# Queries loaded with twelve rows of a head to a partition: a new token order in an attention and gated-MLP kernel

## The chip, the core and the metric

The kernel runs on one core of one Trainium2 chip. The core has engines that run side by side, each with its own queue of instructions in order: TensorE (PE, with weight loads shown as PEld) multiplies matrices into PSUM, VectorE (DVE), ScalarE (ACT) and GpSimd (POOL) work element by element, and SyncE (SP) issues DMAs. ACT and POOL issue some DMAs too. Sixteen DMA engines move the data between HBM and SBUF. The metric is the device time of one execution in microseconds (us).

## The reference

Inputs are float32. q is [8, 16, 384, 64] (batch, query heads, tokens, head width), k and v are [8, 4, 384, 64], so four query heads share a key head. What is computed, per batch:

```python
scores = scale * np.matmul(q, k.transpose(0, 1, 3, 2))     # k, v repeated for 4 query heads
attn = softmax(scores); attn_out = np.matmul(attn, v)
x = attn_out.transpose(0, 2, 1, 3).reshape(B, S, H * D)    # [8, 384, 1024]
h = np.maximum(x @ w_in, 0.0)                              # w_in 1024 x 1024
u, v = h[..., :512], h[..., 512:]
v_n = (v - mean(v)) / sqrt(var(v) + 1e-6)                  # over the last axis
v_s = einsum('ts,bsd->btd', w_spatial, v_n) + b_spatial[None, :, None]   # mixes tokens
out = (u * v_s) @ w_out                                    # [8, 384, 1024]
```

The softmax and the sum over keys do not depend on the order in which keys stand. The token order of the queries is carried through x, h and v_n to the rows of the output, and w_spatial and b_spatial are indexed by it.

## The kernel before

**Tokens.** 384 tokens are three tiles of 128. Every load puts tokens 3p, 3p+1 and 3p+2 of a head in partition p (`(p t) d`, `part`, line 106): one partition then reads 768 contiguous bytes per head. Token tile t holds the tokens 3p+t. The output rows (line 447), the bias and w_spatial (`load_spatial`, `cast_spatial`, lines 498 to 509) use the same order.

**Stages.** A batch is 36 units: six sets s (token tile qt = s // 2, head group j = s % 2), each with three key tiles, and in each unit two matmuls that share the array, one for either half of the head pair (`units`, line 242, matmul at 256). For each, ScalarE takes the exponential into aT (`exp`, line 266); `weigh` (line 270) multiplies by v, with a column of ones for the sums, and VectorE divides (lines 289, 291). x is transposed (`x_turn` on TensorE for the first batches, `x_send` by DMA from batch 2). `gated` (line 455) is a generator of the MLP's matmuls: `v_part` (pv, line 331), `u_part` (pu, 390), `s_part` (psp with wsT16, 409), `o_part` (po, 436, copy to osb, store at 450 or 452). `pour` (line 612) takes these as filling between the attention's units; the Python code thus writes the order of TensorE's queue out by hand. In the first 21 units (`ALONE`, line 631) one unit is emitted at a time, later three.

**The start.** k, q and v are loaded as float32 and cast to float16, then turned by TensorE transposes for batches 0 and 1 (`k_turn`, `q_turn`), by DMA transposes from batch 2 (`k_send`, `q_send`). Lines 124 to 129 issue the first loads: half of the first q tile on ACT's queue, the others on SP's. Lines 533 to 541 are what the engines do first, with groups of matmuls on an identity matrix (`idle`, line 525) between the transposes. Lines 543 to 569 give POOL's order of casts and DMA issues: w_in, the loads of batches 1 and 2, the bias, w_spatial, w_out. `at(n, ...)` hangs work on unit n; lines 570 to 588 hang the first transposes there.

**Queues.** SP issues in order: first loads, the transpose of w_spatial (line 512), then batch by batch the loads, the transposes of k, q and x, and the output stores. `osb` has three buffers, which hold one batch's three token tiles.

Of the kernel before, what the change touches and what calls it, by code (L numbers as in the profile page):

```python
# [9 lines left out]
FP32 = mybir.dt.float32  # L10
# [7 lines left out]
def kernel(  # L18
# [75 lines left out]


    stage = {}

    def stage_tile(n, b, j=None):
        heads = 2 * G if n == "q" else HKV
        t = ld.tile(  # L100
            [P, heads, NT * D], FP32, name=f"{n}32_{b}_{j}", tag=f"{n}32", bufs=4 if n == "q" else 2
        )
        stage[n, b, j] = t
        return t
# [7 lines left out]
    def load_v(b, eng=sp):  # L112
        part(v[b], stage_tile("v", b), 0, HKV, eng)

    def load_q(b, j, eng=sp):
        part(q[b, 8 * j : 8 * j + 8], stage_tile("q", b, j), 0, 2 * G, eng)

# [5 lines left out]
    )  # L123
    part(q[0, 0:8], q00, G, 2 * G, act)
    part(k[0], k0, 0, 2, sp)
    part(q[0, 0:8], q00, 0, G, sp)
    part(k[0], k0, 2, 4, sp)
    part(q[0, 8:16], q01, 0, 2 * G, sp)
    part(v[0], v0, 0, HKV, sp)

    w_in16 = cst.tile([P, NK, DFF], FP16, name="w_in16")
# [41 lines left out]
    def cast_q(b, j, eng, ts=None, hs=(0, 1)):  # L173
        if (b, j) not in q16s:
            q16s[b, j] = ld.tile([P, NT, G, 2, D], FP16, name=f"q16_{b}_{j}", tag="q16", bufs=4)
        t16 = q16s[b, j]
        src = stage["q", b, j].rearrange("p (h i) (t d) -> p h i t d", h=2, t=NT)
        for hh in hs:
            if ts is None:
                eng.tensor_copy(  # L180
                    t16[:, :, :, hh, :].rearrange("p t i d -> p i t d"), src[:, hh]
                )
            else:
                for t in ts:
                    eng.tensor_copy(t16[:, t, :, hh, :], src[:, hh, :, t])

# [55 lines left out]
    def units(u, count):  # L242
# [11 lines left out]
        for kt, hh, sc in sorted(scs, key=lambda x: x[:2]):  # L254
# [3 lines left out]
                kTs[b][rows, j, kt * P : (kt + 1) * P],  # L258
                qTs[b, j][rows, qt, :],
                start=True,  # L260
# [168 lines left out]
    def o_part(b, tt, half):  # L429
# [16 lines left out]
        cols = slice(half * 512, (half + 1) * 512)  # L446
        rows = out[b].rearrange("(p t) d -> p t d", t=NT)
        copy(act if half and (last or tt == 1) else dve, osb[:, cols], po, f"po_{b}_{tt}_{half}")
        if last:
            sp.dma_start(rows[:, tt, cols], osb[:, cols])  # L450
        elif half:
            sp.dma_start(rows[:, tt, :], osb)
        yield C512
# [66 lines left out]
    def at(n, f, *args):  # L520
        todo.setdefault(n, []).append((f, args))
# [47 lines left out]
    send_spatial()  # L569
    at(2, k_turn, 0, 1, dve)  # L570
    for n, b, j, t in (
        (2, 0, 1, 0),
# [10 lines left out]
    ):  # L583
        at(n, q_turn, b, j, t, dve)
    at(15, k_turn, 1, 0, dve)
    at(18, k_turn, 1, 1, dve)
# [127 lines left out]
```

## Time and profile before

| | us |
|---|---|
| median of three runs (244.82 to 245.74) | 244.94 |
| the profiled execution, its own time | 245.65 |
| its span in the trace | 243.5 |
| TensorE busy | 234.7 |
| ScalarE busy | 170.0 |
| VectorE busy | 142.6 |
| GpSimd busy | 99.3 |
| first scores (line 256) | 7.72 |
| last output store issued (line 450) | 240.24 |

The granted TensorE clock was 0.997 of full speed. The profile shows, for each group of instructions, the source line, the engine, out and in tiles, how often it ran, the mean time of one, and what the engine waited for before it. SPq is SP's queue of DMA issues; the time to landing of a DMA runs from its issue to the last byte's signal. q1 is the queue of DMAs that SP issues, q10 that of ACT, q0 that of POOL. A DMA share is the mean busy share of the 16 engines; it can go over 1 where packets of two queues overlap.

### The profile page before, as it was taken

Reading aid. Unit: us, or ns where it says so; the run is one execution under the profiler, and the core shown is the slowest. Engines: PE = TensorE matmul, PEld = TensorE weight load, DVE = VectorE, ACT = ScalarE, POOL = GpSimd, SP = SyncE. Lnnn points to the kernel's source line nnn. Section 1 sums busy time; section 2 is a strip of 40 time slices with the busy share of each in tenths; the row PEclk is TensorE's granted clock in tenths of the full one; section 3 lists DMA queues with packets and bytes.
Section 4 is the critical chain, followed back from the end, with each engine's and each line's share of the span. In section 5 each row is a group of like instructions: output and inputs, shape, how many; then the busy total and the mean of one; then the engine's idle time right before and its main releaser. Section 6 shows DMA issues by size and latency. Waiting matters only on the chain.

```text
span 243.5 us, 5905 instructions
## 1 busy us (share of the span) xinstructions
PE 234.7 (96%) x2334; PEld 126.3 (52%) x2334; DVE 142.6 (59%) x373; ACT 170.0 (70%) x348; POOL 99.3 (41%) x142
## 2 busy tenths in 40 slices
PE   7599999999999999999999999999999999999993
PEld 7355556645564545554555545645555545545541
DVE  1255866567545776367664766456754766467361
ACT  2599977977898868996888856977678866501211
POOL 1699872475042630349005830556003400360520
PEclk9999999999999999999999999999999999999998
DMA  7999999995399959996999399995932334240147
GB/s 218 241 270 285 301 323 204 154 319 195 63 145 264 276 168 215 239 250 223 203 239 265 109 187 247 321 187 113 227 88 43 106 112 132 43 172 3 61 192 265
DMA packets 70651, 46.68 MB, mean 192 GB/s; under 512 B 44912, under 2 KB 65456, under 8 KB 70624
## 3 DMA queue, kind: packets, MB, share of 16 engines
q1 hardware_dynamic: 66016, 37.27, 63.5%
q0 software_dynamic: 4080, 8.65, 14.7%
q8 instruction: 18, 0.29, 0.5%
q10 hardware_dynamic: 528, 0.39, 0.5%
q14 instruction: 9, 0.07, 0.1%
HBM read 25.95 MB, written 12.58 MB: 158 GB/s over the span
## 4 chain that ended last, share of the span: by engine, by line
PE 91%; DMA 3%; DVE 3%; SPq 1%; issue 0%; ACT 0%
PE pu L390 18%; PE po L436 17%; PE pv L331 17%; PE sc L256 15%; PE av L276 14%; PE psp L409 7%; DMA q<-in_q_dram 3%; PE xps L308 1%; PE qps L217 1%; DVE x L291 1%; SPq L107 1%; DVE qT L195 1%; DVE r L289 0%; DVE stats L357 0%; DVE vr L345 0%
## 5 line engine op out<-in xcount | busy, mean ns | idle before, releaser
L268 ACT ACTIVATE aT<-sc 128x512 f16<-128x512 f32 x288 | 148.0, 613 | 36.8 <-PE sc L256 36.2
L276 PEld LDWEIGHTS <-aT 128*128 128x128 f16 x1152 | 47.8, 97 | 17.3 <-issue 1.8
L375 POOL TENSOR_SCALAR vn<-vr,rstd,nmr 128x512 f16<-128x512 f32 x24 | 18.1, 767 | 85.6 <-DVE nmr L370 63.5
L276 PE MATMUL av<-v,aT 128*128 128x65 f16 x1152 | 51.6, 193 | 0.3 <-DVE x L291 0.2
L331 PE MATMUL pv<-w_in,xt 128*128 128x512 f16 x192 | 51.1, 379 | 0.0
L436 PE MATMUL po<-w_out,gT 128*128 128x512 f16 x192 | 50.7, 379 | 0.0
L390 PE MATMUL pu<-xt,w_in 128*128 128x384 f16 x256 | 49.9, 326 | 0.0
L256 PE MATMUL sc<-qT,kT 64*128 64x512 f16 x288 | 42.7, 380 | 0.8 <-DVE qT L195 0.7
L291 DVE TENSOR_TENSOR x<-av,r 128x256 f16<-128x256 f32 x96 | 40.7, 424 | 3.3
L422 POOL TENSOR_TENSOR gT<-vs,uT 128x384 f16<-128x384 f32 x31 | 28.2, 913 | 35.3 <-DVE vs L421 18.0
L289 DVE RECIPROCAL r<-av 128x4 f32<-128x4 f32 x96 | 17.2, 179 | 42.1 <-PE av L276 41.9
L195 DVE COPY osb<-po 128x512 f32<-128x512 f32 x38 | 25.9, 685 | 17.2 <-PE po L436 16.2
L390 PEld LDWEIGHTS <-w_in 128*128 128x128 f16 x256 | 22.1, 97 | 17.1 <-issue 5.5
L401 ACT ACTIVATE uT<-pu 128x384 f16<-128x384 f32 x32 | 15.8, 494 | 16.3 <-PE pu L390 16.2
L436 PEld LDWEIGHTS <-gT 128*128 128x128 f16 x192 | 17.1, 97 | 17.5 <-issue 3.0
L331 PEld LDWEIGHTS <-xt 128*128 128x128 f16 x192 | 16.0, 97 | 17.7 <-issue 5.3
L180 POOL CAST q<-q 128x768 f16<-128x768 f32 x28 | 22.4, 834 | 5.0 <-DMA q<-in_q_dram 4.2
L256 PEld LDWEIGHTS <-kT 64*128 64x128 f16 x288 | 10.8, 94 | 24.9 <-issue 13.5
L409 PE MATMUL psp<-wsT,vn 128*128 128x384 f16 x96 | 22.3, 327 | 0.0
L421 DVE TENSOR_TENSOR vs<-psp,bias_bc 128x384 f32<-128x384 f32 x32 | 17.6, 552 | 6.4 <-PE psp L409 6.3
L345 DVE TENSOR_SCALAR vr<-pv 128x512 f32<-128x512 f32 x24 | 16.4, 682 | 8.4 <-PE pv L331 8.4
L357 DVE BATCH_NORM_STATS2 stats<-vr 128x6 f32<-128x512 f32 x24 | 16.4, 685 | 0.1
(42 smaller groups left out, 100.4 us busy)
## 6 DMA issues: line engine op xcount, KB each, us to landing
out_dram<-osb SPq DMA_DIRECT2D x21, 512.0 KB, 2.7
q<-in_q_dram SPq DMA_DIRECT2D x11, 768.0 KB, 7.7
q<-in_q_dram POOLq DMA_DIRECT2D x4, 768.0 KB, 9.8
v_None<-in_v_dram SPq DMA_DIRECT2D x6, 384.0 KB, 4.5
w_in<-in_moe_w_in_dram POOLq DMA_DIRECT2D x4, 512.0 KB, 8.4
k_None<-in_k_dram SPq DMA_DIRECT2D x5, 384.0 KB, 4.0
out_dram<-osb SPq DMA_DIRECT2D x6, 256.0 KB, 2.4
w_out<-in_moe_w_out_dram POOLq DMA_DIRECT2D x2, 512.0 KB, 14.1
```

The costliest lines, as they stand in the source:

```text
L180: eng.tensor_copy(t16[:, :, :, hh, :].rearrange("p t i d -> p i t d"), src[:, hh])
L195: (act.copy if eng is act else dve.tensor_copy)(o, i)
L256: nc.tensor.matmul(sc, kTs[b][rows, j, kt * P : (kt + 1) * P], qTs[b, j][rows, qt, :], start=True, stop=True,)
L268: act.activation(a, sc, AF.Exp, scale=scale)
L276: nc.tensor.matmul(av[:, i * (D + 1) : (i + 1) * (D + 1)], aT[:, kt, hh, i * P : (i + 1) * P], v1[b % 2][:, 2 * j + hh, kt, 0 : D + 1], st ...
L291: dve.tensor_tensor(x16s[b][:, qt, c : c + 256].rearrange("p (i d) -> p i d", i=G), o[:, :, 0:D], r.to_broadcast([P, G, D]), ALU.mult,)
L331: nc.tensor.matmul(pv, xts[b][:, kt, st * P : (st + 1) * P], w_in16[:, kt, DH:DFF], start=(kt == 0), stop=(kt == NK - 1),)
L375: pool.tensor_scalar(vn, v_r.pop((b, st)), rstd[:, st : st + 1], nmr[:, st : st + 1], op0=ALU.mult, op1=ALU.add,)
L390: nc.tensor.matmul(pu[:, 0:S], w_in16[:, kt, m * P : (m + 1) * P], xts[b][:, kt, :], start=(kt == 0), stop=(kt == NK - 1),)
L409: nc.tensor.matmul(psp[:, 0:S], v_n[b, st][:, m * P : (m + 1) * P], wsT16[:, st, :], start=(st == 0), stop=(st == NT - 1),)
L422: (dve if b == B - 1 and m == NM - 1 else pool).tensor_tensor(gTs[b][:, m, :], vs, uTs[b][:, m, :], ALU.mult)
L436: nc.tensor.matmul(po, gTs[b][:, m, tt * P : (tt + 1) * P], w_out16[:, m, half * 512 : (half + 1) * 512], start=(m == 0), stop=(m == NM - 1),)
```

## The change

Queries get a new layout. Partition (i, c) now holds twelve rows of head i of a group of four: token 12c + 4t + r for t in 0..2 and r in 0..3, so that the whole group of four heads is 128 partitions of 3,072 contiguous bytes. Token tile t of the queries then holds tokens 12c + 4t + r with position (r, c). `part_q` loads any choice of half groups and token tiles: for the first batch, tile 0 of the first and second q tile is loaded ahead of v, and tiles 1 and 2 of both behind v. In the transposed q the columns of a tile stand as (r, i, c); the score matmul reads them in the order (i, r, c), in runs of 32. Keys and values keep their order. The output rows, the bias and w_spatial follow the new token order, so the output's DRAM side is walked as (r, c, d) and w_spatial's as (r, c, t, s).

The order at the start changes too. The group of 18 idle matmuls becomes 8; the cast of the second q tile on VectorE moves behind the second k transpose's copy, with 16 idle matmuls ahead of that q tile's transposes and 8 behind; on POOL the first half load of w_in's second column half and the cast of v are moved ahead of a q cast, and the second half load stands behind that cast.

```diff
     def stage_tile(n, b, j=None):
-        heads = 2 * G if n == "q" else HKV
+        shape = [P, 2, NT, G * D] if n == "q" else [P, HKV, NT * D]
...
+    def part_q(b, j, hs, ts, eng):
+        h0, h1, t0, t1 = hs[0], hs[-1] + 1, ts[0], ts[-1] + 1
+        eng.dma_start(
+            stage["q", b, j][:, h0:h1, t0:t1],
+            q[b, 8 * j + 4 * h0 : 8 * j + 4 * h1].rearrange(
+                "(h i) (c t r) d -> (i c) h t (r d)", i=G, t=NT, r=G
+            )[:, :, t0:t1],
+        )
+
     def load_q(b, j, eng=sp):
-        part(q[b, 8 * j : 8 * j + 8], stage_tile("q", b, j), 0, 2 * G, eng)
+        stage_tile("q", b, j)
+        part_q(b, j, (0, 1), (0, 1, 2), eng)
...
-    part(q[0, 0:8], q00, G, 2 * G, act)
+    part_q(0, 0, (1,), (0,), act)
     part(k[0], k0, 0, 2, sp)
-    part(q[0, 0:8], q00, 0, G, sp)
+    part_q(0, 0, (0,), (0,), sp)
     part(k[0], k0, 2, 4, sp)
-    part(q[0, 8:16], q01, 0, 2 * G, sp)
+    part_q(0, 1, (0, 1), (0,), sp)
     part(v[0], v0, 0, HKV, sp)
+    part_q(0, 0, (0, 1), (1, 2), sp)
+    part_q(0, 1, (0, 1), (1, 2), sp)
...
-        src = stage["q", b, j].rearrange("p (h i) (t d) -> p h i t d", h=2, t=NT)
+        src = stage["q", b, j].rearrange("p h t (r d) -> p h t r d", d=D)
...
-                qTs[b, j][rows, qt, :],
+                qTs[b, j][rows, qt].rearrange("p (r i c) -> p i r c", r=G, i=G),
...
-        rows = out[b].rearrange("(p t) d -> p t d", t=NT)
+        rows = out[b].rearrange("(c t r) d -> t r c d", t=NT, r=G)[tt]
...
-            sp.dma_start(rows[:, tt, cols], osb[:, cols])
+            sp.dma_start(rows[:, :, cols], osb[:, cols])
         elif half:
-            sp.dma_start(rows[:, tt, :], osb)
+            sp.dma_start(rows, osb)
...
-        eng.dma_start(ws32, moe_w_spatial.rearrange("(p t) s -> p t s", t=NT))
+        rows = moe_w_spatial.rearrange("(c t r) s -> r c t s", t=NT, r=G)
+        eng.dma_start(ws32, rows)
...
-            bias_bc.rearrange("a (t p) -> a t p", t=NT), b32.rearrange("a (p t) -> a t p", t=NT)
+            bias_bc.rearrange("a (t r c) -> a t r c", t=NT, r=G),
+            b32.rearrange("a (c t r) -> a t r c", t=NT, r=G),
...
-                ws16[:, :, tt, :], ws32[:, tt].rearrange("p (s t) -> p t s", t=NT)
+                ws16[:, :, tt].rearrange("p s (r c) -> p s r c", r=G),
+                ws32[:, tt].rearrange("p (c s r) -> p s r c", s=NT, r=G),
...
-    idle(18)
+    idle(8)
     q_turn(0, 0, 0, dve)
     idle(8)
 
-    cast_q(0, 1, dve, (0,))
+    load_w_in(1, 0, 4)
+    cast_v(0, pool)
     cast_q(0, 0, pool, (1,))
-    load_w_in(1, 0, 4)
     load_w_in(1, 4, 8)
-    cast_v(0, pool)
     cast_q(0, 1, pool, (1,))
...
     at(2, k_turn, 0, 1, dve)
+    at(2, cast_q, 0, 1, dve, (0,))
+    at(2, idle, 16)
...
+    at(2, idle, 8)
```

More of the change, by code (lines that the diff above doesn't have):

```diff
@@ L98, in stage_tile @@
     def stage_tile(n, b, j=None):
-        heads = 2 * G if n == "q" else HKV
+        shape = [P, 2, NT, G * D] if n == "q" else [P, HKV, NT * D]
         t = ld.tile(
-            [P, heads, NT * D], FP32, name=f"{n}32_{b}_{j}", tag=f"{n}32", bufs=4 if n == "q" else 2
+            shape, FP32, name=f"{n}32_{b}_{j}", tag=f"{n}32", bufs=4 if n == "q" else 2
         )
@@ L176, in cast_q @@
         t16 = q16s[b, j]
-        src = stage["q", b, j].rearrange("p (h i) (t d) -> p h i t d", h=2, t=NT)
+        src = stage["q", b, j].rearrange("p h t (r d) -> p h t r d", d=D)
         for hh in hs:
             if ts is None:
-                eng.tensor_copy(
-                    t16[:, :, :, hh, :].rearrange("p t i d -> p i t d"), src[:, hh]
-                )
+                eng.tensor_copy(t16[:, :, :, hh, :], src[:, hh])
             else:
                 for t in ts:
-                    eng.tensor_copy(t16[:, t, :, hh, :], src[:, hh, :, t])
+                    eng.tensor_copy(t16[:, t, :, hh, :], src[:, hh, t])
     def new_kT(b):
```

## The prediction

> **What bounds the kernel now.** I read the page's busy shares, the chain that ended last and the DMA parts first, then the timeline of the first 12 us, then the DMA queue's own timeline, and at last windows of one batch each.
>
> ```profile
> PE 234.7 (96%) x2334; PEld 126.3 (52%) x2334; DVE 142.6 (59%) x373; ACT 170.0 (70%) x348; POOL 99.3 (41%) x142
> ...
> PE 91%; DMA 3%; DVE 3%; SPq 1%; issue 0%; ACT 0%
> ...
> out_dram<-osb SPq DMA_DIRECT2D x21, 512.0 KB, 2.7
> q<-in_q_dram SPq DMA_DIRECT2D x11, 768.0 KB, 7.7
> ```
>
> TensorE is the bound: busy for 96% of the 243.5 us, and 91% of the chain. Only the start (the DMA share of the chain) and the last stores are not matmuls. The last lines are the loads and stores whose shape this change alters.
>
> The start, from the timeline (start, length, engine, line):
>
> ```profile
> 5.76 0.50 DVE L185 CAST q<-q 128x256 f16<-128x256 f32 x2 [1.58 <-DMA q<-in_q_dram]
> ...
> 7.72 0.82 PE L256 MATMUL sc<-qT,kT 64*128 64x512 f16 x6 [0.16 <-DVE qT L195]
> 8.13 3.04 ACT L268 ACTIVATE aT<-sc 128x512 f16<-128x512 f32 x6 [2.87 <-PE sc L256]
> ...
> 9.98 0.49 DVE L185 CAST q<-q 128x256 f16<-128x256 f32 x2 [2.41 <-DMA q<-in_q_dram]
> 10.39 0.35 DVE L195 COPY kT<-kps 128x384 f16<-128x384 f16 x1
> ...
> 11.87 7.11 ACT L268 ACTIVATE aT<-sc 128x512 f16<-128x512 f32 x14 [0.70 <-PE sc L256]
> ```
>
> Scores begin at 7.72, ScalarE at 8.13. From there to about 31 us ScalarE is nearly full (two exps of 0.51 us per unit), so the first exp sets this stage; its one real gap is 0.70 us, for the second q tile, whose load lands at 9.95.
>
> The end, from the DMA queue's timeline, and the queue's traffic in the window 229.5 to 232.6, which holds the first of these stores:
>
> ```profile
> 229.68 6.11 SPq L452 DMA_DIRECT2D out_dram<-osb  x3
> 236.06 4.51 SPq L450 DMA_DIRECT2D out_dram<-osb  x6
> ```
> ```profile
> q1 hardware_dynamic: 144, 0.52, 42.0%
> ```
>
> Nine stores go out in the last 11 us; the last is issued at 240.24 and lands at 242.3. In the window one store of 512 KB is 128 data packets of 4 KB: 0.42 x 16 engines x 3.1 us / 128 = 0.163 us for one packet on one engine, so 8 packets each, 1.3 us of its 2.6 us to landing. The other 1.3 us is fixed.
>
> One batch each, from the windows (time of each engine; the last two columns are DMA share and GB/s):
>
> ```profile
> 85.00:112.00 27.00, 27.00 (x276) 13.69 (x273) 16.80 (x45) 21.92 (x46) 9.45 (x14) 1.00 0.92 218
> 166.00:193.00 27.00, 27.00 (x273) 14.15 (x271) 16.34 (x43) 20.66 (x44) 8.04 (x11) 1.00 0.56 126
> ```
>
> A batch takes 27 us. Its DMA work fills 0.56 x 27 = 15 us of each DMA engine with stores and transposes alone, 25 us with the loads: hidden, but there is little room.
>
> **The change part by part.**
>
> *Head.* Ahead of the first q cast the old order moves 384 + 192 + 384 KB (landing at 5.74), the new one 128 + 192 + 128. Landings of the old loads follow each other at about 320 KB/us (384 KB from 4.55 to 5.74). The first q tile then lands near 4.2, bounded by a small load's own 2.9 us from issue. K's cast ends by 4.1, the two q casts (0.50) by 4.7. But eight idle matmuls at 0.118 us (18 took 2.13) run until 5.5 behind the k transposes, where 18 ran until 6.67. Four transposes (0.4 to 0.5), the copy (0.42): scores at about 6.5 instead of 7.72, so 1.2 us. The second q tile lands by 5.5. Its cast moves behind the k copy on VectorE, so the copy no longer waits 1.9 us in the queue; 16 idle matmuls (0.076 each when warm: 8 took 0.61) end about when that cast does. The gap of 0.70 shrinks to about 0.3. Head: 1.6 us gained; bounds 0 (DMA contention from w_in, issued two us sooner on POOL) and 2.3 (the whole gap goes too). SP issues two DMAs more, 0.5 us each, behind v: nobody waits for SP before 33 us. POOL's v cast now stands ahead of a q cast and the second w_in issue, which moves from 8.48 to about 10.4; at its old 7.5 us to landing it is there at 18, its first matmul comes at 20.64 less 1.6. The 14 idle matmuls more lie in waits. I take -1.6.
>
> *Casts and transposes* keep their counts and element numbers: nothing. Cover: POOL is 41% busy.
>
> *Scores* read q in runs of 32 columns (64 bytes). No matmul of before reads its moving operand in pieces. Bounds: nothing, or half rate, 144 pairs x the 0.216 us between pairs in the trace = 31 us more. The nearest rows are VectorE's casts that write 64-element pieces, at 0.29 us for 256 elements against 0.55 for 384 unbroken: no price for pieces. I take nothing. The Trainium skill (SBUF — State Buffer, section Door 1: The DMA port swizzle, its note on cachelines) has lines of 16 bytes as the unit; runs of 64 bytes would cost nothing by it, and no run here shows it.
>
> *Stores.* Token order now is (c t r), so a store's rows on the DRAM side are four groups of 32. The programs as built:
>
> ```
> before  L452 DMACopy out_dram<-osb 128x1024
> after   L464 DMACopy out_dram<-osb 4x32x1024
> ```
>
> Every transfer of before, loads too, has 128 as its outermost step and ran on 16 engines; none shows what a step of four does. If a transfer is dealt to engines along its outermost step, four get all of it. Bounds for one store: 8 packets per engine (1.3 us) or 32 (32 x 0.163 = 5.2 us). I take four engines, since the step is what changed and an even deal of 4 cannot reach 16. The Trainium skill states this rule (DMA: Bandwidth & Descriptors, section Why a DMA increments its semaphore by 16 and not by 1): the largest number up to 16 that divides the slowest dimension of both sides; it gives four here, and this trace can neither confirm nor refute it.
>
> Then three things follow, all on the four engines.
>
> (a) The tail. From 229.68 three stores of 5.2 and six half stores of 2.6 make 31.2 us of packets; with 1.3 fixed the last lands at 262.2 instead of 242.3: +20. The three output buffers add nothing, since copies wait only for stores that stand ahead in the same queue.
>
> (b) Batches 2 to 6. A batch's three stores cost these engines 15.6 us instead of 3.9: +11.7 on 22 to 25 us. (22: 15 plus 192 load packets at 0.036; 25: the window's share.) The new q packets of 3 KB save 0.7. So 33 to 36 us of work per 27 us. Transposes measured alone (18 ns per packet of 256 bytes, 432 a batch) bring it down to 30. SP's ring is served in order, so the transposes of q and x land late. In the trace the q transposes land 5.4 to 9.6 us before the scores that read them, x's 4.5 to 25. I walked the SP queue's issue times through one engine's ring with these prices (it gives the old landings within 2.3 us). Landings slip by 6 us at 95, 8 to 12 at 120, 15 at 175, so scores wait from batch 5 on and have lost about 9 us by batch 7. With packets 10% cheaper it is 2, with contended ones 15 or more. I take 8, bounds 0 and 16.
>
> (c) w_spatial, 576 KB, 4x96 rows on POOL's queue. POOL's queue holds the engines for 99.2% of 12 to 45 us, at 8.25 MB / 33 us = 250 KB/us: 2.3 us on 16 engines, 9.2 on four, or 5.9 at a store packet's rate. So it lands 3.6 to 6.9 later than 31.03. Behind it wait POOL's casts of it and of batch 2's k and q, then SP's transpose of it (issued 33.10, landing 44.91 behind w_out), then psp, first at 46.9. Slack is 2.0, less the 1.6 of the head. Cost 0 (if the other twelve engines, freed of this load, run the rest of the queue ahead) to 6.5; I take 4.
>
> Sum: -1.6 + 20 + 8 + 4 = +30.4. The profiled execution took 245.65 (span 243.5, 2.15 around it), 0.7 above the median of 244.94, so about 276 against it and 275 against the median.
>
> **The rivals.**
>
> A. Stores stay on 16 engines: then only the head counts, 244.94 - 1.6 = 243.3, faster. For it: the packets themselves are the same 128 rows. It decides if the last store's time to landing stays under 3 us. Against: the outermost step.
>
> B. Four engines, but only the tail pays: the queue's slack absorbs (b) and most of (c): 244.9 - 1.6 + 20 + 0 to 2 = 263 to 265. For it: slacks of 5 to 10 us, and transposes that were priced while contended. Against: 30 us of work per 27.
>
> C. Broken reads slow the scores: up to 31 us on top, 275 to 306. For it: TensorE has no room; against: nothing in a row.
>
> **How the numbers follow.** Forecast 0.58 (266 to 287), A 0.12, B 0.25, C 0.05. The range of 8 in 10 leaves out A and nearly all of C: 259, a little under B with a better head, to 287, with (b) and (c) at their ends. A change of 0.5% is about what a measurement here can tell: faster 0.09 and same 0.03 both come from A (a head gain under 1.2 us counts as same), slower 0.88.
>
> **What would show it.** Stores: time to landing of L464 at 6.5 us or more instead of 2.7 and far more in the queue, with all else idle after TensorE's last matmul; if 2.7, the forecast falls. (a): 15 to 20 us between the last osb copy and the end, at a DMA share near a quarter. (b): TensorE gaps ahead of sc from batch 4 on, released by a transpose of q or k; none means B. (c): POOL's ws cast waiting for its DMA until 35 or later, and a TensorE gap ahead of psp near 47. Head: first exp at 6.9, next gap 0.3. Scores: 0.38 us each, pairs 0.216 apart; longer means C.

## The result: 30% slower

The changed kernel takes 318.08 us (316.34 to 321.06 in six runs) against 245.34 for the kernel before on the same chip (244.82 to 247.21, six runs): a ratio of 1.295, with a 95% interval of 1.288 to 1.303. The profiled execution took 321.06 us, its span is 318.9. The prediction was 275 us with a range of 259 to 287. The direction was right and so was most of the mechanism, but the size was far off. Where runs of one kernel lie more than 1.5% apart (element_reads below), a ratio is that of the faster runs.

The profile after, from its page: busy shares, TensorE's granted clock and the DMA engines' share in 40 slices of 8 us, the chain that ended last by engine and by line, and the stores.

```profile
PE 247.3 (78%) x2348; PEld 131.6 (41%) x2348; DVE 143.1 (45%) x373; ACT 170.9 (54%) x348; POOL 100.4 (31%) x142
...
PEclk9999995799999599997589989799789999999555
DMA  6999999927999989959787992989932897212221
...
PE 51%; DMA 35%; POOL 3%; DVE 2%; ACT 1%; SPq 1%; issue 1%; DVEq 0%; ACTq 0%; POOLq 0%
DMA qT<-q 13%; PE pv L343 11%; PE po L448 10%; PE pu L402 9%; PE sc L268 8%; PE av L288 8%; DMA ws<-in_moe_w_spatial_dram 7%; PE psp L421 6%; DMA xt<-x 5%; DMA out_dram<-osb 5%; DMA wsT<-ws 3%; DMA q<-in_q_dram 2%; POOL q L197 1%; ACT aT L280 1%; POOL w_in L154 1%
...
out_dram<-osb SPq DMA_DIRECT2D x21, 512.0 KB
```

TensorE falls from 96% of the span to 78%, and from 91% of the chain to 51%; DMA rises from 3% to 35% of the chain. TensorE's own busy time is 12.6 us longer as well: the granted clock falls to 0.5 to 0.8 in slices in and behind the waits, 0.893 in the mean against 0.997. The DMA row ends in twos and ones, about four of 16 engines.

Where the time went is read by comparing, in both traces, when the same matmul begins (after minus before, us):

| up to | difference | the stage's share | predicted |
|---|---|---|---|
| first exp | -1.2 | | |
| first scores of batch 1 | -1.0 | head: -1.0 | -1.6 |
| first pv of batch 1, behind the first psp | +9.9 | (c) w_spatial: +10.9 | +4 |
| first psp of batch 6 | +52.5 | (b) batches 2 to 6: +42.6 | +8 |
| end of the span | +75.4 | (a) tail: +22.9 | +20 |

The waits of the three slow stages in the changed kernel (us in total, times, longest):

```profile
PE sc L268 <- DMA qT<-q: 26.8, 5, 10.9
...
ACT osb L207 <- DMA out_dram<-osb: 16.6, 3, 7.9
...
DVE osb L207 <- DMA out_dram<-osb: 13.2, 3, 4.6
...
POOL ws L521 <- DMA ws<-in_moe_w_spatial_dram: 9.8, 1, 9.8
...
PE psp L421 <- DMA wsT<-ws: 8.5, 1, 8.5
```

The fourth and fifth line are (c): POOL waits 9.8 us for w_spatial, which lands at 41.8 instead of 31.0, and TensorE then waits 8.5 us for its transpose. Of w_spatial's sixteen landing signals twelve have come by 31.8 and the last four between 38.7 and 41.8. The first line is most of the waiting in (b): five times scores wait for the transposed q. The second and third belong to the tail: the copies into osb wait for buffers that four engines are still emptying.

Waits are not all of it. The same stretch (b) in the windows view, first of the kernel before, then of the changed one (length, busy time of PE, PEld, DVE, ACT, POOL, clock, DMA share, GB/s):

```profile
50.87:211.96 161.09, 160.84 (x1646) 84.58 (x1643) 97.37 (x259) 125.98 (x261) 56.90 (x76) 1.00 0.79 183
60.80:264.48 203.68, 171.19 (x1646) 88.99 (x1643) 97.50 (x259) 126.72 (x261) 56.21 (x74) 0.92 1.01 141
```

TensorE does the same 1646 matmuls. Of the 42.6 us it loses here, 32.2 are idle time and 10.4 are slower matmuls: the clock falls to half in a wait and stays there a while behind it (0.50 from 54.56, where the wait of 8.5 us ends, to 59.3). In (c) it is 8.5 us of waiting and 2.4 of clock.

The end, first the DMA queue's timeline (start, length, line), then the window behind the last matmul (length, busy time of PE, PEld, DVE, ACT, POOL, clock, DMA share, GB/s):

```profile
282.20 6.32 SPq L464 DMA_DIRECT2D out_dram<-osb  x3
293.27 13.44 SPq L462 DMA_DIRECT2D out_dram<-osb  x6
```
```profile
293.00:318.90 25.90, 0.00 (x0) 0.00 (x0) 1.62 (x3) 1.39 (x3) 0.00 (x0) 0.54 0.24 93
```

From 293 on nothing but the last copies into osb and the stores is left, at a DMA share of 0.24, 93 GB/s. The Trainium skill (DMA: Bandwidth & Descriptors, section Why a DMA increments its semaphore by 16 and not by 1) gave four engines for a slowest step of four; this share agrees with it.

One wait of (b), from TensorE's timeline, then the DMA queue's own timeline around it, for the changed kernel:

```profile
155.62 1.46 PE L268 MATMUL sc<-qT,kT 64*128 64x512 f16 x6 [10.95 <-DMA qT<-q]
```
```profile
125.96 3.22 SPq L464 DMA_DIRECT2D out_dram<-osb  x2
130.63 8.07 SPq L327 DMA_TRANSPOSE xt<-x  x1
...
143.63 0.56 SPq L464 DMA_DIRECT2D out_dram<-osb  x1
144.31 3.58 SPq L246 DMA_TRANSPOSE qT<-q  x1
147.97 7.91 SPq L327 DMA_TRANSPOSE xt<-x  x1
```

And the same queue of the kernel before, around the same stores:

```profile
106.59 5.00 SPq L452 DMA_DIRECT2D out_dram<-osb  x2
113.23 1.24 SPq L315 DMA_TRANSPOSE xt<-x  x1
```

Issuing one transpose takes 1.24 us before and 8 us after, right behind the stores: SP itself is held, and with it all that stands behind in its queue. The DMA row of the changed kernel's window 129 to 165 (40 slices of 0.9 us) shows the DMA packets meanwhile:

```profile
DMA  9429922222222991989922222342199999989999
```

Two stretches of 7 and 8 us stand at 0.1 to 0.4, mostly 0.2. This row books a packet's whole time in the slice in which it starts, so a low digit says that few packets start there, and not that the other engines are idle. The packets themselves, in the trace, show more: sixteen transpose packets of 256 bytes that started between 132.3 and 133.2 all end between 140.9 and 141.0, after 7.8 to 8.6 us, when the store issued at 128.64 lands (141.1). In the second stretch fifteen that started at 146.0 to 146.2 stay open for 9.1 to 9.3 us, until 155.3, and the store issued at 143.63 lands at 155.5. The median packet of this kind takes 18 ns. So a transpose is held open on the engines until the four have done their store.

The start and the scores, from the timeline:

```profile
6.51 0.82 PE L268 MATMUL sc<-qT,kT 64*128 64x512 f16 x6 [0.16 <-DVE qT L207]
6.92 5.03 ACT L280 ACTIVATE aT<-sc 128x512 f16<-128x512 f32 x10 [1.39 <-PE sc L268]
...
11.03 0.40 PE L229 MATMUL qps<-ident,q 128*128 128x128 f16 x4 [0.96 <-POOL q L197]
```

Scores begin at 6.51 and ScalarE at 6.92; the gap of 0.70 ahead of the second q tile is gone. At 11 us some of this is given back: TensorE waits 0.96 us for POOL's cast of token tile 1, whose load now stands behind v, and on POOL behind the cast of v. The median score matmul takes 0.38 us in both kernels (the mean of the changed one, 0.40, has those at the lower clock), so reading q in runs of 32 columns costs nothing.

### The profile page after: what moved, and what is told of

Read it like the earlier page. It is cut to its first block, busy times and chain, and to the rows that moved or that the text cites. A ratio compares the mean times of both kernels' runs of the same rounds, so it can differ in the third digit from the quotient of the medians.

```text
span 318.9 us, 5938 instructions
## 1 busy us (share of the span) xinstructions
PE 247.3 (78%) x2348; PEld 131.6 (41%) x2348; DVE 143.1 (45%) x373; ACT 170.9 (54%) x348; POOL 100.4 (31%) x142
## 4 chain that ended last, share of the span: by engine, by line
PE 51%; DMA 35%; POOL 3%; DVE 2%; ACT 1%; SPq 1%; issue 1%; DVEq 0%; ACTq 0%; POOLq 0%
DMA qT<-q 13%; PE pv L343 11%; PE po L448 10%; PE pu L402 9%; PE sc L268 8%; PE av L288 8%; DMA ws<-in_moe_w_spatial_dram 7%; PE psp L421 6%; DMA xt<-x 5%; DMA out_dram<-osb 5%; DMA wsT<-ws 3%; DMA q<-in_q_dram 2%; POOL q L197 1%; ACT aT L280 1%; POOL w_in L154 1%
## 5 line engine op out<-in xcount | busy, mean ns | idle before, releaser
L268 PE MATMUL sc<-qT,kT 64*128 64x512 f16 x288 | 45.4, 401 | 27.2 <-DMA qT<-q 26.8
L288 PEld LDWEIGHTS <-aT 128*128 128x128 f16 x1152 | 50.5, 100 | 19.2 <-issue 5.1
L343 PE MATMUL pv<-w_in,xt 128*128 128x512 f16 x192 | 52.7, 389 | 5.5 <-DMA xt<-x 5.5
L288 PE MATMUL av<-v,aT 128*128 128x65 f16 x1152 | 54.1, 198 | 0.2
L402 PE MATMUL pu<-xt,w_in 128*128 128x384 f16 x256 | 53.5, 344 | 0.0
L434 POOL TENSOR_TENSOR gT<-vs,uT 128x384 f16<-128x384 f32 x31 | 28.3, 912 | 47.6 <-DVE vs L433 24.8
L268 PEld LDWEIGHTS <-kT 64*128 64x128 f16 x288 | 11.6, 96 | 52.2 <-issue 37.8
L402 PEld LDWEIGHTS <-w_in 128*128 128x128 f16 x256 | 23.0, 101 | 19.7 <-issue 8.9
L421 PE MATMUL psp<-wsT,vn 128*128 128x384 f16 x96 | 24.3, 351 | 8.5 <-DMA wsT<-ws 8.5
L207 ACT COPY osb<-po 128x512 f32<-128x512 f32 x10 | 5.9, 591 | 25.1 <-DMA out_dram<-osb 16.6
```

The source lines that it names most:

```text
L207: (act.copy if eng is act else dve.tensor_copy)(o, i)
L268: nc.tensor.matmul(sc, kTs[b][rows, j, kt * P : (kt + 1) * P], qTs[b, j][rows, qt].rearrange("p (r i c) -> p i r c", r=G, i=G), start=True ...
L288: nc.tensor.matmul(av[:, i * (D + 1) : (i + 1) * (D + 1)], aT[:, kt, hh, i * P : (i + 1) * P], v1[b % 2][:, 2 * j + hh, kt, 0 : D + 1], st ...
L343: nc.tensor.matmul(pv, xts[b][:, kt, st * P : (st + 1) * P], w_in16[:, kt, DH:DFF], start=(kt == 0), stop=(kt == NK - 1),)
L402: nc.tensor.matmul(pu[:, 0:S], w_in16[:, kt, m * P : (m + 1) * P], xts[b][:, kt, :], start=(kt == 0), stop=(kt == NK - 1),)
L421: nc.tensor.matmul(psp[:, 0:S], v_n[b, st][:, m * P : (m + 1) * P], wsT16[:, st, :], start=(st == 0), stop=(st == NT - 1),)
```

## The experiments

Each kernel was compared with runs of the kernel before on the same chip, whose medians were 245.0 to 246.0. The last three columns come from the same comparison of traces as above (kernel minus before): up to the first psp or pv behind it, the batches from there to the first psp of batch 6, and the tail. The start varies by 1 to 2 us from run to run, also in kernels whose start is that of before. split_stores, split_ws, the three before_r kernels, near_r16, act_stores and few_loads were run once, so it is their stages that are compared, not their medians; near_r4 took 300.1 to 311.6 us in four runs, and its stages are those of a run of 310.53.

| kernel | median, us | up to pv of batch 1 | batches | tail |
|---|---|---|---|---|
| the change | 318.08 | +9.9 | +42.6 | +22.9 |
| split_both | 255.22 | +1.9 | +0.1 | +7.5 |
| split_stores | 261.02 | +8.2 | +0.1 | +7.4 |
| split_ws | 306.31 | +0.5 | +37.2 | +22.9 |
| before_r16 | 249.4 | +1.6 | 0.0 | +2.2 |
| before_r8 | 263.39 | +1.8 | +6.4 | +9.5 |
| before_r4 | 304.49 | -0.4 | +36.2 | +23.0 |
| near_r16 | 247.15 | -0.8 | 0.0 | +2.3 |
| near_r4 | 307.97 | +1.4 | +40.5 | +23.0 |
| act_stores | 303.13 | +2.5 | +32.1 | +22.9 |
| few_loads | 292.93 | +0.1 | +24.4 | +22.8 |
| mended | 250.79 | +1.7 | +0.1 | +4.9 |
| reordered | 244.66 | -1.35 | 0.0 | -0.1 |

### Is it the step of four, and whose: split_both, split_stores, split_ws

The theory is that the two transfers with an outermost step of four carry the whole loss. The rival is that something else in the change (the score reads, the order in the head, the loads) has a part in it. The edit writes each such transfer as four DMAs of 32 partitions, either for both or for one of the two:

```diff
-            sp.dma_start(rows, osb)
+            for r in range(G):
+                sp.dma_start(rows[r], osb[r * 32 : (r + 1) * 32])
...
-        eng.dma_start(ws32, rows)
+        for r in range(G):
+            eng.dma_start(ws32[r * 32 : (r + 1) * 32], rows[r])
```

> The changed kernel, with each output store issued as four DMAs of 32 partitions (outermost step 32 on both sides) and w_spatial loaded the same way; nothing else differs. Theory (the outermost step of four is the whole loss): the 75 us of the change go, the head's 1 us of gain stays, SP issues 81 DMAs more at 0.33 us, which costs up to 2 us in the tail: 243.5 to 247 us. Rival (rows scattered over HBM, the strided score reads or the new start cause part of the loss): a loss of 10 us or more stays, 255 us or more.

> The changed kernel with only the stores split in four DMAs; w_spatial stays one load with an outermost step of four. Theory: the 10.9 us that the changed kernel lost ahead of psp of batch 0 come back, against the run with both split: 263 to 267 us, its cast waiting for the load until after 38 us. Rival (that loss came from the stores): 254 to 257 us.

> The changed kernel with only w_spatial split in four loads; stores stay on an outermost step of four. Theory: the changed kernel's time less 10.9: 304 to 310 us, no wait ahead of psp of batch 0. Rival (the late start of batch 2 is what piles the stores up): under 295 us.

With both split, nothing is left of (b) and (c). 255.22 us is a ratio of 1.039 (1.032 to 1.046), 8 us above the upper end of the theory; by the time alone it would be the rival's (255 us or more), and only the stages speak against that. The 10 us that are left sit in two places. The tail costs 7.5, since SP now issues 36 DMAs where nine stood; from the DMA queue's timeline of split_both:

```profile
231.70 7.73 SPq L466 DMA_DIRECT2D out_dram<-osb  x12
239.53 11.17 SPq L463 DMA_DIRECT2D out_dram<-osb  x24
```

That is 0.47 us for each of the last 24, and it ends at 250.7, where the six of before end at 240.6 (2 us of that come from the start). The other place is the start: with w_spatial as four DMAs on POOL's queue, TensorE waits 1.8 us for POOL's casts of q. split_ws has that wait too, with a start of only +0.5; in split_both's profile TensorE also came to its full clock late (its first six score matmuls take 1.47 us, 0.82 in the changed kernel).

With one of the two split, the other's loss stays. From the waits of split_stores, then of split_ws:

```profile
PE psp L421 <- DMA wsT<-ws: 7.7, 1, 7.7
```
```profile
PE sc L268 <- DMA qT<-q: 27.2, 6, 10.5
```

The w_spatial load alone costs 7.9 us up to the first psp and 9.2 up to the matmuls behind it; the stores alone cost 37.2 in the batches and 22.9 in the tail. That is 69.3 of the change's 76.4 us beyond the start. The other 7, 5.4 of them in the batches, appear with both; kernels with the same kind of store differ by 4 us there (before_r4 and near_r4), so whether the two losses add to more than their sum is not shown. split_ws lies in its theory's range, so a late start of batch 2 isn't what piles the stores up; split_stores lies 2 us below its own, with the wait that it expected.

### The number of engines alone: before_r16, before_r8, before_r4

The kernel before, with the store's rows walked as r groups (r = 4 is shown; the others have 8 and 16). It has none of the change's loads, reads or casts.

```diff
-        rows = out[b].rearrange("(p t) d -> p t d", t=NT)
+        rows = out[b].rearrange("(c t r) d -> t r c d", t=NT, r=4)[tt]
...
-            sp.dma_start(rows[:, tt, :], osb)
+            sp.dma_start(rows, osb)
```

> The kernel before, where only the output stores change: they walk the DRAM rows as 16 groups of 8, so the rows of a token tile land permuted in the output. Theory (what counts is how many steps the outermost loop has): 16 engines, as before, 245 to 246 us, store packets near 0.16 us. Rival (any store whose rows are not one even step is slow): 300 us, like four groups.

> The same with 8 groups of 16 rows (rows permuted in the output). Theory: 8 engines; 16 packets of 4 KB on each, 2.6 us a store, tail 3 x 2.6 + 6 x 1.3 = 15.7 us from 229.7, so 4 us more there and nothing in the batches: 248 to 252 us; up to 258 if packets take 0.3 us as at the start of the changed kernel's stores. Rival (uneven rows): 300 us.

> The same with 4 groups of 32 rows (rows permuted in the output), so the stores have the changed kernel's DRAM pattern and nothing else of the change. Theory: the 43 us that the changed kernel loses in batches 2 to 7 and the 23 us in the tail appear here without the rest: 305 to 315 us. Rival (loss comes from the combination with the new q loads or w_spatial): under 290 us.

How many engines a store uses can be counted in the trace by its landing signals: sixteen with 16 groups, eight with eight and four with four (with eight and four, one more comes about 1 us after the issue, ahead of the data).

16, 8 and 4 groups cost 0, 6.4 and 36.2 us in the batches, and 2.2, 9.5 and 23.0 in the tail. before_r4 is the change's (a) and (b) in a kernel that is otherwise the old one. Two expectations were missed: 16 groups were to cost nothing at all, and eight nothing in the batches and 258 us at the most. The loss in the batches is not in proportion to the groups: half the engines cost a sixth of what a quarter of them costs.

The time of one store from issue to its last landing signal, where it is alone in the queue, is 2.60 us in the kernel before, 3.70 with 16 groups, 6.0 with eight and 10.2 with four. For the groups that is about 1.5 us and 0.27 us for each packet of 4 KB that an engine gets (8, 16, 32). The packets' own times in the trace are 0.235 to 0.248 us in the mean. The prediction had 1.3 us and 0.163.

### Are the rows too far apart in DRAM: near_r16, near_r4

With 16 groups the same 16 engines move the same packets, but a store takes 3.70 us instead of 2.60. One candidate is the address: a group's rows lie 192 KB apart (48 KB with four groups), 12 KB in the kernel before. These two kernels keep the groups and put a group's rows one behind the other (r = 4 is shown):

```diff
-        rows = out[b].rearrange("(p t) d -> p t d", t=NT)
+        rows = out[b].rearrange("(r t c) d -> t r c d", t=NT, r=4)[tt]
```

> The same with 16 groups of 8 rows, a group's rows one behind the other (the output's rows are permuted). With the rows of a group 192 KB apart (16 groups as well) a lone store took 3.70 us against 2.60 before, both on 16 engines. Theory of the addresses: 2.6 us for a lone store, and the time of the kernel before within 1.5 us of start variation (243.5 to 247). Theory that the two-step form of the list costs by itself: 3.7 us and +2 us in the tail (247 to 249.5).

> The kernel before, with stores that walk the output's rows in four groups of 32 as in the change, but with the 32 rows of a group one right behind the other in DRAM (rows (r t c) in place of (c t r)); the output's rows are permuted by it. The kernel with four groups whose rows lie 48 KB apart took 304.5 us, +36.2 in batches 2 to 6 and +23 behind the last value, and a lone store of it took 10.2 us (250.09 to 260.27), its first 4 us at 12 to 13 packets a microsecond of some 300 ns, the rest at 25 of 159 ns. Theory of the addresses (rows that lie far apart make the early packets slow): all packets take 159 ns, a lone store takes 32 x 159 ns and the 1.5 us from issue to first packet, 6.5 us; the batches cost nearer to the 8 us of the prediction (0 to 16) and the tail 15 to 18: 265 to 278 us. Theory of the four engines alone: the same lone store of 10 us and 300 to 308 us.

The addresses are not it: a lone store still takes 3.7 us with 16 groups and 10.3 with four, and near_r4 loses no less than before_r4. From the DMA queues in the window 228.8 to 232.6 of near_r16, which holds one store (and one issue behind it):

```profile
q1 hardware_dynamic: 144, 0.52, 51.5%
...
out_dram<-osb SPq DMA_DIRECT2D x2, 512.0 KB, 3.7
```

This is the view from which the prediction took its packet, with the same 128 data packets: 0.515 x 16 x 3.8 / 128 = 0.245 us each, against 0.163 in the kernel before. In the trace of before_r16 the middle half of such a store's first 64 packets take 296 to 382 ns, and the last 64 take 159 in the median. Why the grouped list runs slower at first stays open; it is neither the number of engines (16 in both) nor the rows' distance.

Two figures say how much this price is worth. It is that of a store that finds its engines free: in the change's tail the first store has 0.236 us a packet and keeps four engines for 7.8 us, the two right behind it have 0.159 from the first packet on (5.1 us for the second). In the change's batches the mean of all stores is 0.204. And by itself it costs the batches nothing: before_r16 has 0.253 there, and a loss of 0.0.

### Is it the order of SP's queue: act_stores

The transposes stand behind the stores in SP's queue. This kernel issues the stores, still in four groups, from ScalarE's queue, one output part later; w_spatial is split.

```diff
+        if unsent:
+            d, x = unsent.pop()
+            act.dma_start(d, x)
...
-            sp.dma_start(rows[:, :, cols], osb[:, cols])
+            act.dma_start(rows[:, :, cols], osb[:, cols])
...
-            sp.dma_start(rows, osb)
+            unsent.append((rows, osb))
```

> The changed kernel with w_spatial as four DMAs of 32 partitions (all 16 engines; with that alone it took 306.3 us, +37.2 in batches 2 to 6, +22.9 behind the last value) and with the stores, still on a step of four, issued from ScalarE's queue, a whole tile's store one output part later, so that SP's queue holds transposes and loads alone. Theory of SP's queue (a store whose four engines are busy holds up the issue of the transposes behind it): the batches cost 0 to 10, the tail 23 as before: 268 to 282 us. Theory of the engines (transposes spread over 16 engines end with the slowest four, whichever queue they come from): +30 to +40 in the batches, 300 to 312 us. ScalarE's own price is 27 issues by 0.55 us, 15 us over 243, of which I expect 0 to 5 in the time.

The batches still cost 32.1 us, against 37.2 in split_ws, the same kernel with the stores on SP. From TensorE's waits in act_stores, then from SP's queue:

```profile
PE pv L343 <- DMA xt<-x: 11.5, 2, 7.6
PE sc L268 <- DMA qT<-q: 10.7, 2, 6.7
```
```profile
119.47 13.90 SPq L327 DMA_TRANSPOSE xt<-x  x2
```

The waits move in part from q's transpose to x's, and that is all. Issuing two transposes still takes 13.9 us, with no store in SP's queue. So at most 5 us are due to the queue's order. It fits the packets above: a transpose is spread over all engines and isn't done before the four have done their part, whichever queue it came from.

### Occupancy or the length of one store: few_loads

```diff
         if b > 2:
-            at(u0 - 24, load_k, b)
-            at(u0 - 24, load_v, b)
-            at(u0 - 22, load_q, b, 0)
-            at(u0 - 20, load_q, b, 1)
+            for n, j in (("k", None), ("v", None), ("q", 0), ("q", 1)):
+                stage[n, b, j] = stage[n, 2, j]
```

> The kernel before with stores in four groups of 32 rows (304.5 us; +36.2 in batches 2 to 6, +23 behind the last value), and with the loads of q, k and v of batches 3 to 7 left out: those batches compute with batch 2's (the output's rows are permuted too). Theory of occupancy: in a batch of the kernel before the 16 DMA engines are busy 0.97 of 27.15 us, 26.3 us each, of which 67.7 us of store packets by 16, 4.2 us. On four engines these are 16.9, so those four have 26.3 - 4.2 + 16.9 = 39 us a batch, 12 over the period. The loads' packets are 128.9 us by 16, 8.1 us an engine: without them 31 us, 4 over, a third, so +10 to +18 in the batches and 278 to 286 us. Theory of the store's length alone (each transpose waits out the 10 us store ahead of it, whatever else moves): +30 to +37, 298 to 305 us.

This stands on top of before_r4; the loads of batches 3 to 7 are left out, and those batches compute with batch 2's.

The batches cost 24.4 us, between the two expectations (10 to 18, and 30 to 37). A third of before_r4's 36.2 goes with the loads, so the length of one store alone isn't the reason. Of TensorE's idle time alone three quarters stay, 19.2 of 24.8 us. The engines' sum of work isn't the reason by itself either. The expectation had a packet of 0.176 us; in the batches the trace has 0.193 in before_r4 and 0.210 in few_loads. With these the same sum gives 26.3 - 4.2 + 3 x 32 x 0.193 = 40.6 us a batch for before_r4, 13.5 over the period of 27.15, and 26.3 - 4.2 - 8.1 + 3 x 32 x 0.210 = 34.2, 7 over, without the loads. Half the loss would stay, and five batches with 13.5 us each would lose 67 where 36.2 were lost. How much of (b) is work on the four engines, and how much is transposes that wait out a store, these runs do not tell apart.

### Other ways to reorder: element_reads, exp_writes

If the tokens of a tile stand as (c, r) instead of (r, c), the outermost step of a store and of w_spatial is 32, and they are on 16 engines again. The order then has to be made elsewhere: in the score matmul's reads, in single elements of 2 bytes that lie 256 bytes apart, or in the exponential's writes, in elements that lie 8 bytes apart.

```diff
-                qTs[b, j][rows, qt].rearrange("p (r i c) -> p i r c", r=G, i=G),
+                qTs[b, j][rows, qt].rearrange("p (r i c) -> p i c r", r=G, i=G),
...
-        rows = out[b].rearrange("(c t r) d -> t r c d", t=NT, r=G)[tt]
+        rows = out[b].rearrange("(c t r) d -> t c r d", t=NT, r=G)[tt]
...
-        rows = moe_w_spatial.rearrange("(c t r) s -> r c t s", t=NT, r=G)
-        eng.dma_start(ws32, rows)
+        rows = moe_w_spatial.rearrange("(c t r) s -> c r t s", t=NT, r=G)
+        for tt in range(NT):
+            eng.dma_start(ws32[:, tt], rows[:, :, tt])
```

That is element_reads, with the bias and the cast of w_spatial in the same order. exp_writes keeps its last two edits, reads the scores as the change does, and reorders in the exponential:

```diff
-        return [(aTs[b, s][:, kt, hh], sc, f"sc_{b}_{s}_{hh}_{kt}") for kt, hh, sc in scs]
+        return [(aTs[b, s][:, kt, hh].rearrange("p (i c r) -> p i r c", r=G, i=G), sc, f"sc_{b}_{s}_{hh}_{kt}") for kt, hh, sc in scs]
...
-        act.activation(a, sc, AF.Exp, scale=scale)
+        act.activation(a, sc.rearrange("p (i r c) -> p i r c", r=G, i=G), AF.Exp, scale=scale)
```

> The changed kernel with the columns of a query tile read in the order (i, c, r), one element at a time 256 bytes apart, so that position in a tile is (c, r): a store is one DMA again, with an outermost step of 32 on the DRAM side (and w_spatial three loads with 32 outermost). Theory (the outermost step is the whole loss, and the place of the reads is free): 243.5 to 247 us, the last store landing under 3 us after its issue. Rival (single elements slow the matmul's reads): pairs of score matmuls more than 0.216 us apart, 275 us or more.

> The same token order and the same stores, but the reorder from (i, r, c) to (i, c, r) is made where ScalarE writes the exponentials: 2-byte elements 8 bytes apart, while the scores read runs of 32 as in the changed kernel. Theory: 243.5 to 247 us. Rival (scattered writes slow ScalarE): exps over 0.51 us in the first stage; at 0.6 us the first 21 units take 4 us longer, 248 us or more.

The stores are back to 3.0 us to landing in both, and both kernels are slower than the change, as their rivals had it: 356.5 and 358.8 us in the two faster runs of element_reads (ratio 1.456, 1.446 to 1.466; its profile is of a run of 363.83) and 389.33 us (1.583, 1.575 to 1.591). The groups of the score matmuls in element_reads, and of the exponentials in exp_writes (busy us, mean ns):

```profile
L268 PE MATMUL sc<-qT,kT 64*128 64x512 f16 x288 | 134.8, 1031 | 0.2 <-DVE qT L207 0.2
```
```profile
L280 ACT ACTIVATE aT<-sc 128x512 f16<-128x512 f32 x288 | 334.3, 1430 | 2.5 <-PE sc L268 2.5
```

A score matmul takes 1031 ns instead of 380, an exponential 1430 instead of 611. So the change's runs of 64 bytes are free, and single elements are far from it. The Trainium skill (SBUF — State Buffer, section Door 1: The DMA port swizzle, its note on cachelines) asks for at least two accesses to a line of 16 bytes. The score reads agree with it: 32 elements in a run are free, and one to a line takes 1031 ns. The exponential's writes do not: two of them in a row fall into each line of 16 bytes, and they take 1430 ns instead of 611.

### A version that keeps the gain: mended, reordered

mended is split_both with two repairs: SP issues w_spatial behind its first loads, and the last batch stores whole tiles, halves only for its last tile, on two queues.

```diff
-        eng.dma_start(ws32, rows)
+        for r in range(G):
+            sp.dma_start(ws32[r * 32 : (r + 1) * 32], rows[r])
...
-        if last:
-            sp.dma_start(rows[:, :, cols], osb[:, cols])
-        elif half:
-            sp.dma_start(rows, osb)
+        if last and tt == NT - 1:
+            for r in range(G):
+                eng = act if half and r % 2 else sp
+                eng.dma_start(rows[r][:, cols], osb[r * 32 : (r + 1) * 32, cols])
+        if half and not (last and tt == NT - 1):
+            for r in range(G):
+                sp.dma_start(rows[r], osb[r * 32 : (r + 1) * 32])
```

> The changed kernel with all of it kept in the loads and reads, each store as four DMAs of 32 partitions, w_spatial as four DMAs issued by SP behind its first loads (POOL no longer issues them), and in the last batch whole-tile stores for two tiles, halves for the last one alone, whose second half two queues share. Every extra of the steps of four should go: batches 0, tail +0 to +1.5 (four issues of 0.5 us where one stood), w_spatial 0, head -1.5 to +1. Theory: 243.5 to 247 us, not to be told from the kernel before. A rival, by which the change's head is worth its 2 us once POOL isn't held by w_spatial's issues: 242 to 243.5.

250.79 us, a ratio of 1.020 (1.016 to 1.024), 3.8 us above the upper end of what was expected. From TensorE's waits, then the DMA queue's timeline of mended:

```profile
PE pv L343 <- DMA w_in<-in_moe_w_in_dram: 2.0, 1, 2.0
```
```profile
231.47 11.81 SPq L468 DMA_DIRECT2D out_dram<-osb  x20
244.76 2.86 SPq L465 DMA_DIRECT2D out_dram<-osb  x6
```

w_spatial, issued by SP from 4.3 us on, now stands beside the first half of w_in, issued at 6.0; TensorE waits 2 us for w_in, which it did not in the change. In the tail SP is still issuing the second tile's four DMAs when the last tile's copies are done.

reordered goes back from the new token order inside the MLP. The changed order has token 12c + 4t + r at column 32(4t + r) + c of a row of tokens; the old order wants token 12c + 3k + t at position 4c + k of tile t. Both count the twelve tokens of a c, so one strided view leads from one to the other, and ScalarE's Relu, which reads that row from PSUM anyway, can take it. Stores, the load of w_spatial and the bias are then those of the kernel before.

```diff
-        act.activation(uTs[b][:, m, :], pu[:, 0:S], AF.Relu)
+        act.activation(
+            uTs[b][:, m, :].rearrange("p (t c k) -> p t c k", t=NT, k=G),
+            pu[:, 0:S].rearrange("p (k t c) -> p t c k", t=NT, k=G),
+            AF.Relu,
+        )
```

> The changed kernel's loads of q, strided score reads, order in the head and idle matmuls, but with the stores, w_spatial's load and the bias of the kernel before (128 rows of 12 KB steps, one DMA each): the one place where tokens go from the new order to the old is ScalarE's Relu, which reads its 384 columns of PSUM in steps of 96 (t c k out of k t c). All extras of the steps of four go. If ScalarE reads PSUM in steps at no cost (494 ns a Relu, as before): the time is before's plus the head alone, -1.6 by the prediction with start variation of 1 to 2 us: 243 to 246 us. If the steps cost what its scattered writes did (1302 ns against 550): 32 x 0.8 = 26 us more of ScalarE beside 171 of 243, some of it in the way of psp: 246 to 256 us.

244.66 us (12 runs) against 245.52 (17 runs): a ratio of 0.9971 (0.9947 to 0.9994), a small gain whose interval leaves out 1. From the page of reordered: the chain, and the Relu's group, with that of the kernel before below it.

```profile
PE 93%; DVE 3%; DMA 1%; issue 0%; ACT 0%
...
L413 ACT ACTIVATE uT<-pu 128x384 f16<-128x384 f32 x32 | 15.8, 494 | 16.3 <-PE pu L402 16.2
```
```profile
L401 ACT ACTIVATE uT<-pu 128x384 f16<-128x384 f32 x32 | 15.8, 494 | 16.3 <-PE pu L390 16.2
```

The strided Relu takes 494 ns, as before. In its profile all markers stand 1.35 us earlier from the first scores of batch 1 to the last matmul, and the span ends 1.4 us earlier.

## Why the prediction was wrong

**Four engines: right.** The transfers whose outermost step became four went through a quarter of the engines, and undoing just that (split_both) took away (b), (c) and two thirds of (a). Rival A falls with it, and rival B with (b). Rival C falls too: the reads of 64 bytes cost nothing.

**(a), the tail: right.** +20 was predicted and +22.9 measured, from a DMA share near a quarter as described. The price of 0.163 us a packet held for stores right behind another one (0.159); most of the difference is the first store, 7.8 us of packets instead of 5.2. The copies did wait for buffers, up to 7.9 us, but as the text said this added nothing, since the four engines had packets without a break.

**(b), the batches: the term that failed, +8 predicted and +42.6 measured** (36.2 and 37.2 where the stores were the only such transfer). The walk through one engine's ring took 5.2 us for a store ("32 x 0.163 = 5.2 us") and 18 ns for each transpose packet, as "measured alone", which made 30 us of work a batch, and it counted waits alone. The runs show three things in its place.

- A store cost its engines more. The 0.163 came from a store whose list was plain; in the change's batches a grouped one had 0.204 us a packet, 6.5 us in all, and 7.8 alone. The walk reacted strongly to just this price, as the text said for changes of 10%. The ends of (b), 0 and 16, stood for packets 10% cheaper and for contended ones, though no row of before showed a grouped list, so none bounded its price.
- Transposes did not run beside a store at their own rate. Their packets took 65 ns in the mean of the batches (28 before); most still took 18, but one in a hundred over 1 us, up to 9.3, until the store ended. SP was held for up to 8.1 us by one of them (3.1 before).
- TensorE's clock, which the sum leaves out, took 10.4 of the 42.6 us. The waits that the walk meant to forecast as 8 were 32.2.

That the queue's order is not the reason is shown by act_stores. How the 32.2 us of waits divide between dearer stores and held transposes is not shown: the price alone costs nothing on 16 engines (before_r16), the loss grows from 6.4 to 36.2 us between eight engines and four, and in few_loads more stays than the sum of work would leave. A smaller reading was off as well: the q transposes land 4.4 to 9.6 us ahead of their scores in the kernel before, not 5.4 to 9.6.

**(c), w_spatial: mis-sized as well, +4 against +10.9** (9.2 alone, in split_stores). It was expected 3.6 to 6.9 us later than before and landed 10.8 later. The way that would have cost nothing, with the other twelve engines running ahead, did not happen: they had their part by 31.8, and POOL and SP behind it still waited for the four. Why the four took longer than either of the two rates is not shown. The consequence was the one described: POOL's cast waits, then the transpose, then psp (8.5 us), and 2.4 us of slower clock on top.

**The head: right in direction, a little too large.** -1.6 was predicted. In reordered, where nothing else is in the way, the profile has -1.35 and the runs' ratio puts the whole gain at 0.7 us (0.1 to 1.3). In the changed kernel -1.0 reached batch 1, with 0.96 us lost at POOL's cast at 11 us: the prediction named v's cast and w_in's issue that now stand ahead of a q cast on POOL, but priced only the w_in that they delay, not the q cast.

## What to carry to other kernels

When a new layout changes the shape of a DMA's list, look at its outermost step on both sides before anything else: a step of four put a 512 KB store on a quarter of the engines, and it held up every transpose behind it. Price such a transfer from a row with the same form of list, and what runs beside it from a row in which both run; if there is none, let the range say so. In a stage whose engines are 0.97 full, the loss grows much faster than the price. Count the slower clock behind each wait as well. A new order can often be ended where an engine already reads PSUM: one strided view on the Relu cost nothing and left all DMAs as they were.

## What the runs showed of the hardware

- A store in groups that finds its engines free is slower than a plain one on the same 16 engines: 3.70 against 2.60 us for 128 rows of 4 KB, 0.244 us a packet against 0.161 (before_r16). Right behind another store it is not: 0.159 (the change's tail). The rows' distance in DRAM, 4 KB or 192 KB, made no difference.
- While four engines work off a store, transposes behind it come to a halt: SP's issue of one takes 8 us instead of 1.24, and sixteen packets of 256 bytes stay open until the store ends. Most still take 18 ns; about 1% take 0.9 to 9.3 us, and none more than 2.4 us in the kernel before.
- A low digit in the DMA row means that few packets start, not that engines are idle: the row stood at 0.2 while sixteen transpose packets were open for 8 us.
- TensorE's clock stays at half for a while behind a wait: 0.50 for the 4.7 us behind the wait that ended at 54.56. In the batches this cost a third as much as the waits (10.4 and 32.2 us).
- TensorE reads a moving operand in runs of 64 bytes at full speed (0.38 us for 512 columns), and in single elements of 2 bytes at 1.03 us.
- ScalarE writes float16 elements 8 bytes apart at 1.43 us for 512 columns, against 0.61 in a row, but reads float32 from PSUM in steps of 384 bytes at no cost (494 ns for 384 columns in both).
